# More blocks of 512 rows: 21 singles, 48 pairs, then 22 blocks of four units, 18 of them beside the remaining conv and route work

## The chip, the cores and the metric

The kernel runs on one NeuronCore of a Trainium2 chip. A core has a matrix engine (TensorE, PE in the profile), a vector engine (VectorE, DVE), an activation engine (ScalarE, ACT), a general engine [...] (GpSimd, POOL), and SyncE (SP), which issues the plain DMAs. [...] The metric is device time in microseconds. Everything is float32.

## What is computed

The input is 8 sequences of 3,584 rows with 192 channels, 28,672 rows in all. First comes a causal convolution along the sequence with 7 taps and 8 heads of 24 channels; each head's taps are a softmax of its 7 weights. Then each row goes to one of 8 experts:

```python
logits = x @ w_gate; local_gate = sigmoid(x @ w_local)
for each row s of a sequence:
    fresh = argmax(logits[s])
    e = fresh if s == 0 or local_gate[s] < 0.5 else previous e
    p = softmax(logits[s])
    out[s] = p[e] * (relu(x[s] @ w1[e]) @ w2[e])
```

`w1[e]` is 192 x 1024 and `w2[e]` 1024 x 192. A row whose local gate is not below 0.5 keeps the expert of the row before it, so the expert is a scan along the sequence.

## The kernel before

**Groups and slots.** The rows are handled in 16 groups of 1,792 (`PT`, `NPART`). For a group, conv makes the convolved rows `y_sb` (one ScalarE multiply for the first tap of a head, six VectorE multiply-adds for the others, L401 and L411). Route then computes logits, experts, probabilities and, for each row, its slot in a DRAM table `slots`, in which every expert has a region of its own. Groups 0 and 1 are done in a faster way with matmuls at the start (`wide`, `wide_route`). Each group's rows are scattered to their slots by 14 indirect DMAs of 128 rows (`put`, L801) that GpSimd issues; 16 of them for groups 0 and 1.

**Blocks.** The expert network runs over blocks of rows of one expert. A unit is 128 rows (`UT`). A block has one unit ("single"), two ("pair", `BT`) or four (`QT`, 512 rows). While groups are still arriving, the kernel takes as many full blocks as the rows that have arrived must yield whatever their experts are (`_sure`), and a bit more in the late stages (`_likely`). The lists `ONE` and `TWO` say up to which block each group serves: 35 singles, all from groups 0 to 2 (`EARLY = 3`), then 60 pairs from groups 3 to 12 (`PAIRED = 60`). After the last group come 13 blocks of four, 4 late pairs, 14 late singles that take what is left of each expert, and spare blocks, which are run only when a planned block found no rows. `FIRST` is the number of the first block of four, 95. The tables that say which expert and which unit a block has are computed on VectorE (`table`, `tables`) and read by SyncE (`entry`).

**One block.** SyncE loads the expert's weights, 1.5 MB, three blocks ahead (`load_w`, four buffers), and the rows of the block from the slots (`load_rows`). TensorE transposes the rows (`turn`, L383), ScalarE copies them to SBUF; TensorE does the hidden product (`hidden`, L999), ScalarE applies relu; TensorE does the second product (`output`, L1016), ScalarE and VectorE scale and add its two halves (L1024, L1030), and GpSimd scatters the rows to `out` (L1034). TensorE's order is: hidden of this block, transposes of the next, output of this block.

**Blocks of four.** Their hidden product (`seven`, L1152) is a two-by-two scheme of Strassen's kind over two row halves and two of the three 64-channel thirds: 7 products in place of 8, with the remaining third done plainly, so 11 half-size products in place of 12. It needs sums of weights (`combine_w`, four on GpSimd) and of rows (`combine_x`, five on VectorE), three copies out of PSUM on ScalarE (h11, h22, h12), and three sums of 128 x 1,024 on VectorE (L1166, L1169, L1179). The second product (`output_late`, L1196) has two parts of 256 rows. In this stage PSUM is divided anew: the pools of the pair stage are closed (`banks.close()`), and three double banks `late_p` take their place. The buffers for xT, the combinations and h come from the conv's input and row tiles (`make_room`), since conv is over by then.

**Side work.** Conv and route of the coming groups are written as Python generators that yield an assumed cost after each instruction. Between the parts of a block the kernel calls `step(time)`, which adds instructions of route, or of conv where there is no route work or route has yielded "hop", until the assumed costs add up to `time`: for a pair 4.8 after the hidden product, 1.2 within the output and 3.6 after it. `ensure(i)` issues the row loads of up to three blocks ahead; while a group that block needs is not routed or not fully scattered, and the block is at most two ahead, it adds a step of 4.2 and a `put` at once. Elsewhere `put(ins)` makes GpSimd wait for the instruction `ins` ("anchor"), which spaces the scatters.

Of the kernel before, what the change touches and what calls it, by code (L numbers as in the profile page):

```python
# [17 lines left out]
P = 128  # L18
# [28 lines left out]
EARLY = 3  # L47
# [17 lines left out]
PAIRED = 60  # L65
LEFT4 = E * (QT // 2 + UT // 8)
LEFT2 = E * (BT // 2 + UT // 8)
# [3 lines left out]
PAST = ONE[-1] * UT + TWO[-1] * BT  # L71
FOUR = _likely(N - PAST, QT, LEFT4)
LOST = FOUR - _sure(N - PAST, QT)
# [7 lines left out]
REST = NU - ONE[-1] - 2 * TWO[-1] - 4 * FOUR - 2 * PAIRS + LOSE  # L81
# [21 lines left out]
def kernel(  # L103
# [14 lines left out]
    ys = ctx.enter_context(tc.tile_pool(name="ys", bufs=4))  # L118
# [5 lines left out]
    hp = ctx.enter_context(tc.tile_pool(name="hp", bufs=1))  # L124
    op = ctx.enter_context(tc.tile_pool(name="op", bufs=2))
# [244 lines left out]
    tab = [cst.tile([P, 3], F32, name=f"tab{k}") for k in range(5)]  # L370
    ends = [cst.tile([P, 1 + E], F32, name=f"ends{k}") for k in range(5)]
    for k in range(5):
        nc.gpsimd.memset(tab[k], 0.0)
        nc.gpsimd.memset(ends[k], 0.0)
# [12 lines left out]
    def row_tile():  # L387
        return ys.tile([P, NB, DG], F32, name="y_sb")

    def conv(g, x_sb):  # L390
        y_sb = row_tile()[:, :NT, :]
# [197 lines left out]
    def logits(g, y_sb):  # L589
# [6 lines left out]
        yield "hop"  # L596


        lps = [hps_p.tile([P, TQ * Q], F32, name="hps") for half in range(2)]
# [15 lines left out]
        for r in range(4):  # L615
            for j in range(4):
                t, u = TQ * j, min(TQ * (j + 1), NT)
                at = r // 2 * TQ + t - begin[j]
                e0 = r % 2 * (E + 1)
                nc.vector.tensor_copy(lt[Q * r:Q * r + Q, t:u, :],  # L620
                                      lq[Q * j:Q * j + Q, at:at + u - t, e0:e0 + E + 1])
                yield 0.12
        return lt

    def route(g):
# [62 lines left out]
        krow = sm.tile([1, 2, P], F32, name="krow")  # L688
# [89 lines left out]
    def tables(g):  # L778
        if ONE[g] > (ONE[g - 1] if g else 0):
            yield from table(0, g, 1, ONE[g])  # L780
        if TWO[g] > (TWO[g - 1] if g else 0):
            yield from table(1, g, 2, TWO[g])
        if g == LAST:
            yield from table(2, g, 4, FOUR, 0)
            yield from table(3, g, 2, PAIRS, 0)
            yield from table(4, g, 1, None)
            yield from fill(g)
# [133 lines left out]
    blocks += [(2, 4, i, LAST) for i in range(FOUR)]  # L921
    blocks += [(3, 2, i, LAST) for i in range(PAIRS)]
    blocks += [(4, 1, i, PADS) for i in range(REST)]

# [39 lines left out]
    def turn(n, xg):  # L964
# [9 lines left out]
        xT = tp.tile([P, KD, BT], F32, name="xT")  # L974
# [13 lines left out]
    def hidden(n, wb, xT, shares=(1, 1)):  # L988
# [4 lines left out]
        for two in range(2):  # L993
            hps = [hps_p.tile([P, 2, BT], F32, name="hps") for half in range(2)]
            for d in range(KD):
                for j in range(2):
                    f0 = (d * 4 + two * 2 + j) * P
                    for half, rows in halves():
                        nc.tensor.matmul(hps[half][:, j, w], lhsT=wb[rows, f0:f0 + P],  # L999
                                         rhs=xT[rows, d, w], start=(d == 0 and j == 0),  # L1000
                                         stop=(d == KD - 1), skip_group_check=True)
# [3 lines left out]
            for _ in range(shares[two] if n == KT else (0, sum(shares))[two]):  # L1005
# [3 lines left out]
    def output(n, wb, xg, hT):  # L1009

        yps = [yps_p.tile([P, 512], F32, name="yps") for half in range(2)]
        for m4 in ([0, 1, 4, 5], [2, 3, 6, 7]):
            for k in range(n):
                for m in m4:
                    for half, rows in halves():
                        nc.tensor.matmul(yps[half][:, k * D:(k + 1) * D],  # L1016
                                         lhsT=hT[rows, m, k * P:(k + 1) * P],
                                         rhs=wb[rows, WA + m * D:WA + (m + 1) * D],
                                         start=(m == 0 and k == 0), stop=(m == FK - 1),
                                         skip_group_check=True)  # L1020
        o_sb = op.tile([P, KT, D], F32, name="o_sb")
        y = [[yps[half][:, k * D:(k + 1) * D] for half in range(2)] for k in range(n)]
        for k in range(n):
            half = nc.scalar.activation(o_sb[:, k, :], y[k][0], Act.Copy, scale=xg[:, k, 0:1])  # L1024
        if n == KT and len(to_put) > NT - 2:
            put(half)

        step(1.2 if n > 1 or st["block"] else 0)
        for k in range(n):
# [3 lines left out]
            nc.gpsimd.nop()  # L1033
            sent = nc.gpsimd.indirect_dma_start(  # L1034
                out=out, in_=o_sb[:, k, :], in_offset=None,
                out_offset=bass.IndirectOffsetOnAxis(ap=xg.bitcast(I32)[:, k, IX:], axis=0),
                bounds_check=N - 1, oob_is_err=False)
            tc.declare_no_dep(sent.ins, group="sent", reason="each token has one slot")
            tc.add_to_no_dep_group("sent", sent.ins)
# [4 lines left out]
    def ring(i):  # L1044

        if "rows" not in room:
            room["rows"] = row_tile().rearrange("p b d -> p (b d)")
# [3 lines left out]
    def make_room():  # L1051

        one, two = [xs.tile([P, NX, D], F32, name="x_sb").rearrange("p t d -> p (t d)")
                    for _ in range(2)]
        three = row_tile().rearrange("p b d -> p (b d)")
        for name, flat, at, size in (("xT", one, 0, KD * QT), ("xc", one, KD * QT, 4 * HU * P),
                                     ("wt", one, KD * QT + 4 * HU * P, 6 * P),
                                     ("h0", two, 0, 4 * HU * P), ("h1", two, 4 * HU * P, 4 * HU * P),
                                     ("h2", two, 8 * HU * P, 4 * HU * P), ("h3", three, 0, 4 * HU * P)):
            room[name] = flat[:, at:at + size]  # L1060
# [13 lines left out]
    def turn_in(n, at):  # L1074
        xT = room["xT"][:, :KD * n * P].rearrange("p (d s) -> p d s", d=KD)
# [34 lines left out]
    def combine_w(wb):  # L1110


        wt = room["wt"].rearrange("p (k s) -> p k s", k=3)
# [396 lines left out]
```

## Time and profile before

| | us |
|---|---|
| median of 3 runs | 1322.66 (1322.0 to 1323.66) |
| the profiled execution, its own time | 1305.35 |
| its span | 1303.6 |
| TensorE busy (matmul) | 1284.2 |
| VectorE busy | 846.3 |
| ScalarE busy | 651.1 |
| GpSimd busy | 523.1 |
| first block of four starts at | 910.24 |
| last block of four ends at | 1175.6 |

The span is from the first to the last instruction; the profiled execution's own time has 1.75 us more around it. Busy time of TensorE is modelled, so 99% does not mean that each matmul runs at its peak. The page's slices divide the span in 40 parts of 32.6 us with the busy share in tenths. Line numbers are those of the kernel before.

### The profile page before, as it was taken

The page shows a single profiled execution, that of the slowest core. Times are in us where ns is not written, and L with a number is a line of the kernel's source. Part 1 is how long each engine was busy: PE and PEld are TensorE (multiplying, and loading weights), DVE is VectorE, ACT ScalarE, POOL GpSimd, SP SyncE. Part 2 cuts the span into 40 slices and gives each one's busy share as a digit, 9 for nine tenths or more (in the row PEclk, how much of TensorE's full clock was granted, in tenths as well). Part 3 has the DMA queues.
Part 4 walks back from the last instruction along what each step waited for, and adds up shares of the span by engine and source line. Part 5 has one row for each costly group of instructions (what it writes and reads, how often), then busy time and mean ns, then how long its engine had stood idle before and what let it go on. Part 6 is the DMA issues. An engine that isn't in the chain of part 4 may idle for free.

```text
span 1303.6 us, 40830 instructions
## 1 busy us (share of the span) xinstructions
PE 1284.2 (99%) x16434; PEld 1220.6 (94%) x16434; DVE 846.3 (65%) x2526; ACT 651.1 (50%) x1482; POOL 523.1 (40%) x577
## 2 busy tenths in 40 slices
PE   9899999999999999999999999999999999999997
PEld 7799999999999999999999999999999999999997
DVE  5989898988988899998999996801333333330000
ACT  5456565544445445444454544444645556454453
POOL 3455353533435344353544534454433433322211
PEclk9999999999999999999999999999999999999999
DMA  5799999975757576575765755666323323324584
GB/s 195 285 357 415 386 384 345 398 273 202 269 203 278 196 274 244 207 280 190 281 246 204 281 193 205 214 213 235 128 87 135 122 105 140 110 94 167 212 303 164
DMA packets 63077, 300.42 MB, mean 230 GB/s; under 512 B 12064, under 2 KB 34263, under 8 KB 45474
## 3 DMA queue, kind: packets, MB, share of 16 engines
q1 hardware_dynamic: 40560, 252.54, 53.2%
q0 software_dynamic: 22320, 45.22, 9.5%
q8 instruction: 131, 2.15, 0.7%
q14 instruction: 64, 0.52, 0.1%
q10 hardware_dynamic: 2, 0.00, 0.0%
HBM read 252.12 MB, written 46.07 MB: 229 GB/s over the span
## 4 chain that ended last, share of the span: by engine, by line
PE 96%; DVE 3%; issue 0%; POOL 0%; POOLq 0%; ACT 0%; DVEq 0%
PE yps L1016 31%; PE hps L999 31%; PE ps L1196 15%; PE ps L1152 8%; PE ps L1103 4%; PE xps L383 2%; PE xps L1152 2%; PE hps L604 2%; DVE y_sb L411 1%; PE hps L233 1%; PE hps L178 0%; DVE hot L574 0%; PE hps L256 0%; PE yps L264 0%; DVE run L475 0%
## 5 line engine op out<-in xcount | busy, mean ns | idle before, releaser
L1016 PE MATMUL yps<-wb,hT 64*128 64x192 f32 x4960 | 429.8, 325 | 3.2 <-DVE o_sb L1030 2.4
L999 PE MATMUL hps<-xT,wb 64*128 64x256 f32 (+1 forms) x4560 | 425.9, 338 | 1.9 <-DVE at L503 1.2
L999 PEld LDWEIGHTS hps<-xT,wb 64*128 64x128 f32 x4560 | 378.7, 188 | 33.9 <-issue 3.9
L1016 PEld LDWEIGHTS yps<-wb,hT 64*128 64x128 f32 x4960 | 405.7, 187 | 4.6 <-DVE o_sb L1030 2.7
L411 DVE SCALAR_TENSOR_TENSOR y_sb<-x_sb,c,y_sb 128x336 f32<-128x336 f32 x672 | 375.6, 569 | 28.4 <-ACT y_sb L401 10.5
L801 POOL DMA_INDIRECT slots<-y_sb,posi x228 | 229.6, 1007 | 205.7 <-ACT xT L985 90.8
L1004 ACT ACTIVATE hT<-hps 128x512 f32<-128x512 f32 (+1 forms) x380 | 176.4, 516 | 244.5 <-PE hps L999 244.5
L1034 POOL DMA_INDIRECT out_dram<-o_sb,xg x155 | 161.5, 1042 | 276.0 <-DVE o_sb L1030 222.2
L1209 DVE SCALAR_TENSOR_TENSOR o_sb<-ps,y_sb,o_sb 128x192 f32<-128x192 f32 x74 | 28.1, 413 | 233.5 <-ACT o_sb L1206 233.5
L1214 POOL DMA_INDIRECT out_dram<-o_sb,y_sb x74 | 76.4, 1032 | 237.5 <-DVE o_sb L1209 218.7
L1196 PE MATMUL ps<-wb,x_sb 64*128 64x192 f32 x1952 | 165.0, 323 | 0.0
L1196 PEld LDWEIGHTS ps<-wb,x_sb 64*128 64x128 f32 x1952 | 159.3, 187 | 0.6
L1024 ACT ACTIVATE o_sb<-yps,xg 128x192 f32<-128x192 f32 x155 | 58.7, 418 | 178.4 <-PE yps L1016 178.3
L985 ACT COPY xT<-xps 128x256 f32<-128x256 f32 (+3 forms) x380 | 142.0, 374 | 10.6 <-PE xps L383 4.8
L1030 DVE SCALAR_TENSOR_TENSOR o_sb<-yps,xg,o_sb 128x192 f32<-128x192 f32 x155 | 58.6, 410 | 77.2 <-ACT o_sb L1024 77.0
L1206 ACT ACTIVATE o_sb<-ps,y_sb 128x192 f32<-128x192 f32 x74 | 27.9, 418 | 102.2 <-PE ps L1196 97.7
L1152 PE MATMUL ps<-x_sb,wb 64*128 64x256 f32 x624 | 73.7, 376 | 0.0
L1152 PEld LDWEIGHTS ps<-x_sb,wb 64*128 64x128 f32 x624 | 59.0, 187 | 7.3
L401 ACT ACTIVATE y_sb<-x_sb,c 128x336 f32<-128x336 f32 x112 | 61.9, 578 | 0.0
L1103 PE MATMUL ps<-x_sb,wb 64*128 64x128 f32 (+1 forms) x864 | 61.6, 295 | 0.0
L1103 PEld LDWEIGHTS ps<-x_sb,wb 64*128 64x128 f32 x864 | 59.4, 188 | 0.9 <-issue 0.2
L1083 ACT COPY x_sb<-xps 128x128 f32<-128x128 f32 (+5 forms) x124 | 58.7, 473 | 2.3
(277 smaller groups left out, 1043.5 us busy)
## 6 DMA issues: line engine op xcount, KB each, us to landing
wb<-in_w_dram SPq DMA_DIRECT2D x122, 1536.0 KB
x_sb<-in_x_dram SPq DMA_DIRECT2D x14, 1920.0 KB
xg<-slots SPq DMA_DIRECT2D x60, 195.0 KB
wb<-in_w_dram SPq DMA_DIRECT2D x12, 512.0 KB
y_sb<-slots SPq DMA_DIRECT2D x13, 390.0 KB
slots<-y_sb,posi POOLq DMA_INDIRECT x228
xg<-slots SPq DMA_DIRECT2D x33, 97.5 KB
x_sb<-in_xb_dram SPq DMA_DIRECT2D x4, 768.0 KB
```

The lines of the kernel that those rows point to most:

```text
L401: nc.scalar.activation(cols(h), chans(h, 0), Act.Copy, scale=c[:, h, 0:1])
L411: nc.vector.scalar_tensor_tensor(cols(h), chans(h, k), c[:, h, k:k + 1], cols(h), Alu.mult, Alu.add)
L801: ins = nc.gpsimd.indirect_dma_start(out=slots[:, :], in_=rows, in_offset=None, out_offset=bass.IndirectOffsetOnAxis(ap=to, axis=0)).ins
L985: copied = nc.scalar.copy(a, b)
L999: nc.tensor.matmul(hps[half][:, j, w], lhsT=wb[rows, f0:f0 + P], rhs=xT[rows, d, w], start=(d == 0 and j == 0), stop=(d == KD - 1), skip_g ...
L1004: relu = nc.scalar.activation(hT[:, m:m + 2, w], hps[half][:, :, w], Act.Relu)
L1016: nc.tensor.matmul(yps[half][:, k * D:(k + 1) * D], lhsT=hT[rows, m, k * P:(k + 1) * P], rhs=wb[rows, WA + m * D:WA + (m + 1) * D], start= ...
L1034: sent = nc.gpsimd.indirect_dma_start(out=out, in_=o_sb[:, k, :], in_offset=None, out_offset=bass.IndirectOffsetOnAxis(ap=xg.bitcast(I32)[ ...
L1103: nc.tensor.matmul(hps[:, half, j, :], lhsT=wb[rows, f0:f0 + P], rhs=xT[rows, d, :], start=(d == 0 and j == 0), stop=(d == KD - 1), skip_g ...
L1152: ins = nc.tensor.matmul(to[:, half, j, :], lhsT=b[rows, j * P:(j + 1) * P], rhs=a[rows, :], start=(first and j == 0), stop=True, skip_gro ...
L1196: ins = nc.tensor.matmul(yps[:, half, k * D:(k + 1) * D], lhsT=h[two][rows, side, j, k * P:(k + 1) * P], rhs=wb[rows, WA + f * D:WA + (f + ...
L1214: sent = nc.gpsimd.indirect_dma_start(out=out, in_=o_sb[:, k, :], in_offset=None, out_offset=bass.IndirectOffsetOnAxis(ap=xg.bitcast(I32)[ ...
```

## The change

The plan of blocks changes. `EARLY` goes from 3 to 2 and `PAIRED` from 60 to 48, so there are 21 singles (groups 0 and 1) and 48 pairs (groups 2 to 9). A new list `MID` gives 18 blocks of four from groups 10 to 14, with a table of their own (kind 2), and only 4 of the blocks of four wait for the last group. After them come 5 late pairs and 14 late singles. The whole is 21 + 48 + 22 + 5 + 14 blocks in place of 35 + 60 + 13 + 4 + 14. `FIRST` is 69.

Conv and route of groups 13 to 15 are therefore still under way in the stage of blocks of four. `step` is called there too, with the shares `SIDE = (2.4, 4.6, 1.7, 1.5)`: ahead of the h11 sum, after the transposed copies, and after the row scaling on ScalarE in parts 0 and 1. Route's logits on TensorE are then put between parts 0 and 1 and use the bank `late_p[0]`; a new yield "pe" holds them back until such a place comes, and there are none in the last pair ahead of that stage. The overrun of a step is carried to the next (`over`). The 16 small copies of logits into `lt` move from VectorE to ScalarE, four at a time with a "hop" after each four. The order of the built program has these four ScalarE copies between the row scaling of part 1 and the next block's h11 copy three times.

The second row scatter of a pair, or of each part of a block of four, is no longer issued at once: it is kept in `held` and issued with an anchor on a later TensorE instruction. Some scatters to `slots` get other anchors. Row loads in a block of four are issued inside `seven` (`rows_then`).

Buffers: the row tiles `ys` become four named pools, three of them used from group 8 on, so that the fourth holds the rows of the blocks of four; xT has one pool for all stages; h comes from the tile `hot` of the start; the combinations come from five row tiles `xg` and, for two of them, from `hT` after its last use (`more_room`).

```diff
-EARLY = 3
+EARLY = 2
-PAIRED = 60
+NARROW = 8
+PAIRED = 48
+LEFTM = E * (QT // 2 + UT // 2)
+MID = [_likely((g + 1) * PT - PAST, QT, LEFTM) if TWO[g] == TWO[-1] else 0
+       for g in range(LAST)]
+PAST += MID[LAST] * QT
...
+    def row_tile(g):
+        at = g % 4 if g < NARROW else (g + 1) % 3
+        return ys[at].tile([P, NB, DG], F32, name="y_sb")
...
-        yield "hop"
-        lps = [hps_p.tile([P, TQ * Q], F32, name="hps") for half in range(2)]
+        yield "pe"
+        if late_p:
+            both = st["bank"].tile([P, 2, 512], F32, name="ps")
+            lps = [both[:, half, :TQ * Q] for half in range(2)]
+        else:
+            lps = [hps_p.tile([P, TQ * Q], F32, name="hps") for half in range(2)]
...
-                nc.vector.tensor_copy(lt[Q * r:Q * r + Q, t:u, :],
-                                      lq[Q * j:Q * j + Q, at:at + u - t, e0:e0 + E + 1])
-                yield 0.12
+                nc.scalar.copy(lt[Q * r:Q * r + Q, t:u, :],
+                               lq[Q * j:Q * j + Q, at:at + u - t, e0:e0 + E + 1])
+            yield "hop"
...
+        if MID[g] > (MID[g - 1] if g else 0):
+            yield from table(2, g, 4, MID[g], MID[g - 1])
...
+                        if held and d:
+                            held.pop(0)(ins)
...
+            if k == 0:
+                deliver(o_sb[:, 0, :], xg, 0)
+            else:
+                held.append(lambda ins, k=k: deliver(o_sb[:, k, :], xg, k, ins))
...
+        if behind is not None:
+            tc.add_manual_dep(sent.ins, behind.ins.name, SYNC, reason="scatters apart")
...
-        times(yb, s1, t1, True)
+        ins = times(yb, s1, t1, True)
+        if held:
+            held.pop(0)(ins)
+        rows_then()
...
         times(wbk, a13, b31)
+        if st["block"] > FIRST:
+            step(SIDE[0], early=1)
         nc.vector.tensor_tensor(h11, wbk, h11, op=Alu.add)
...
+            if n == KQ:
+                step(SIDE[2 + part], late_p[0] if part == 0 else None)
...
+        if st["due"]:
+            go = (not late_p and st["block"] < FIRST - 1
+                  or bank is not None and (force or st["since"] < st["block"]))
...
+        time += st["over"]
...
             while st["routed"] < g or any(p[0] <= g for p in to_put):
                 if j > i + 2:
                     return
-                step(4.2)
+                if st["routed"] < g:
+                    step(4.2, late_p[0] if late_p else None, force=True)
                 put()
...
+        if n == KQ:
+            step(SIDE[1])
```

## The prediction

> **What bounds the kernel now.** I read the page first: busy shares, the slices, the chain that ended last. Then the TensorE timeline in three windows, then every engine inside one block of 512 rows.
>
> ```profile
> PE 1284.2 (99%) x16434; PEld 1220.6 (94%) x16434; DVE 846.3 (65%) x2526; ACT 651.1 (50%) x1482; POOL 523.1 (40%) x577
> ...
> PE   9899999999999999999999999999999999999997
> ...
> DVE  5989898988988899998999996801333333330000
> ...
> PE 96%; DVE 3%; issue 0%; POOL 0%; POOLq 0%; ACT 0%; DVEq 0%
> ```
>
> TensorE sets the end from slice 2 to the last. VectorE is close behind it for 24 slices (conv and route) and nearly free afterwards. So a change is worth the TensorE time it removes, less the new waits it puts in front of TensorE. What one block costs is the distance between equal lines of the TensorE timeline: singles, pairs, blocks of 512.
>
> ```profile
> 103.42 2.86 PE L999 MATMUL hps<-xT,wb 64*128 64x128 f32 x48
> ...
> 108.87 2.86 PE L999 MATMUL hps<-xT,wb 64*128 64x128 f32 x48
> ...
> 790.90 5.35 PE L999 MATMUL hps<-xT,wb 64*128 64x256 f32 x48
> ...
> 801.56 5.34 PE L999 MATMUL hps<-xT,wb 64*128 64x256 f32 x48
> ...
> 930.66 2.75 PE L1152 MATMUL ps<-x_sb,wb 64*128 64x256 f32 x24
> ...
> 951.08 2.75 PE L1152 MATMUL ps<-x_sb,wb 64*128 64x256 f32 x24
> ```
>
> A single is 5.445 us (four of them from 92.53 to 114.31), a pair 10.67, a block of 512 rows 20.42 against 21.34 for two pairs: it makes 11 products where plain multiplication makes 12. The last view is the inside of such a block (its start is 971.49).
>
> ```profile
> 972.62 1.01 ACT L1158 COPY x_sb<-ps 128x1024 f32<-128x1024 f32 x1 [0.18 <-PE ps L1152]
> ...
> 974.08 1.03 PE L1152 MATMUL ps<-x_sb 64*128 64x256 f32 x8
> ...
> 976.96 1.22 DVE L1166 TENSOR_TENSOR x_sb<-xps,x_sb 128x1024 f32<-128x1024 f32 x1 [3.74 <-PE xps L1152]
> ...
> 978.17 1.23 DVE L1169 TENSOR_TENSOR y_sb<-ps,y_sb 128x1024 f32<-128x1024 f32 x1
> ...
> 979.26 0.63 PE L383 MATMUL xps<-ident,y_sb 64*128 64x64 f32 x16
> ...
> 979.73 1.08 PE L1152 MATMUL ps<-x_sb 64*128 64x256 f32 x8
> ```
>
> Three handovers are narrow. ScalarE's copy of h11 ends at 973.63, and the product into that bank starts at 974.08: 0.45 us to spare. VectorE's h11 sum ends at 978.18, before the transposes at 979.26: 1.08. Its h22 sum ends at 979.40, before 979.73: 0.33. Today nothing else runs on those engines then; after the change conv and route do.
>
> [...] an early row load issued at 53.98 freed TensorE at 56.03, and the scatter whose row ends at 80.45 released its reader only at 87.20, 6.75 us later, with the DMA engines full. [...]
>
> **The change, part by part.**
>
> *Blocks.* 14 singles go (35 to 21), 12 pairs go (60 to 48), 9 blocks of 512 come (13 to 22), one late pair comes (4 to 5). Rows agree: 1,792 + 3,072 = 4,608 + 256. TensorE: −14×5.445 − 12×10.67 + 9×20.42 + 10.67 = −76.2 − 128.0 + 183.8 + 10.7 = **−9.8 us**. The 14 logits passes on TensorE (1.7 us each) stay.
>
> *Blocks that find no rows.* An expert table with too few full units would give an empty block of 20.42 us. Worked out on the given inputs, groups 10 to 14 offer 5, 9, 13, 14 and 20 blocks against 4, 7, 11, 14 and 18 planned: none is empty. 0.
>
> *Side work beside the blocks of 512.* VectorE per block of 512: its own 3×1.22 + 5×0.44 + 4×0.41 = 7.5; side work by SIDE 10.2 units, some 17 conv ops of 0.585 (7 ops took 4.07 at 655.10), 9.9. Sum 17.4 of 20.42. Followed in order: h12 sum ends 9.2 after the block's start; 11 conv ops to 15.6; row sums of part 0 ready at 16.2, done 16.9; five combinations to 19.1; three conv ops to 20.9; next block: row sums to 1.7, four conv ops to 4.1; the h11 sum is due at 5.5. It is idle again 1.4 us before the narrow place, so the cover holds. If not, each us late beyond 0.33 is a us of TensorE. I take 1.0 us for the whole stage (18 blocks, and the first, where conv stands between the combinations and the last pair's row sums); bounds 0 and 9 (one conv op of 0.585 ahead of the sum, in 15 blocks).
>
> *Logits copies on ScalarE.* Per group 16 copies leave VectorE (3.47 us at 649.72). On ScalarE the trace has none; [...] the nearest row (ls, 128x128) is 0.27. In the built order four of them stand between the row scaling of part 1 and the h11 copy in three blocks (groups 13, 14, 15): [...] 0.5 each, **+1.5 us**; bounds 1.3 and 2.0. Before singles and pairs they stand behind the transposed copies, with over 1 us free on ScalarE (2.76 idle at 670.29): 0.
>
> *EARLY 2.* Pairs start at row 2,688, so rows of group 3 are needed from row 3,456 in place of 4,480. In the built order nine scatters of group 3 still wait when block 22 begins, and are issued without an anchor, one after the other, because block 24's rows need them all. GpSimd, from the start T of block 22: row scatter of block 21 at T+1.35 (263.30 to 264.65 in this trace), 0.99 long, gap 0.30; nine at 1.25 pitch (29.81, 31.06, 32.30) end at T+13.6. [...] load and its landing 2.05: T+17.7. TensorE turns these rows at T+10.67+5.18 = T+15.85. Wait 1.8; I take **+2.2** for SP's issue. Bounds: 0.8 (landing in 1) and 6.5 (landing in 6.75). Behind SP's waiting load stand block 25's rows and weights; the weights go out about T+17 for use at T+34, after some 4 us: no second wait. Behind the nine on GpSimd is block 21's second row scatter, which nobody needs before block 23's row scaling. Block 29 has six: [...] bounds 0 and 2.8.
>
> *Spaced scatters, pools, pair steps.* The second scatter of a block now waits on GpSimd for a TensorE instruction. GpSimd in a full block of 512: up to six puts and four scatters at 1.27 and four combinations at 0.75, 15.7 of 20.42; weight combinations end about 18.5 after the block's start, first used 21.3 after. The ring's row loads have three blocks. Hand-over to the new stage without logits in the last pair, transposed tile from its own pool, combination buffers from free row tiles: 0, covered by the same slack.
>
> Sum: −9.8 + 2.2 + 1.5 + 1.0 = **−5.1 us**. The profiled execution took 1305.35, its span 1303.6; the span becomes 1298.5. The median of the runs is 1322.66, 17.3 above the profiled one; that gap I cannot place and carry over: **1317.5 us**, −0.39%. About 0.2% (2.6 us) is what a measurement of this kernel can tell from no change.
>
> **Rivals.**
> 1. *Full gain.* The nine scatters land in time, copies slip through: −9.8 + 0.3, 1313.2. For: the waits view lists only 10 us for TensorE in the whole run. Against: T+17.7 is past T+15.85.
> 2. *Landing under load.* Scatters land in 6.75: 6.5 at block 22, 2.8 at block 29; −9.8 + 9.3 + 2.5 = +2.0, 1324.7. For: the 6.75 was in the single stage, which ends one block before. Against: SP holds weight loads back meanwhile, so the queues empty.
> 3. *Slower: VectorE late for the h11 sum.* If two conv ops (1.17) stand ahead of it when the bank is ready, the h22 sum is 0.84 past its slack; over 15 blocks 12.6, with the 3.7 above: +6.5, 1329.2. It decides from 0.41 us a block ((9.8−3.7)/15). For: VectorE at 85% of the block, three narrow handovers. Against: the 1.4 us counted above.
> 4. *It does not do what it says* (empty blocks): 20.42 each; excluded by the count, 0.
>
> **How the numbers follow.** Forecast 0.48 (own range 1315 to 1320), rival 1 0.20, rival 2 0.18, rival 3 0.14. Faster by over 0.2%: 0.48 + 0.20 = 0.68. Within: 0.18 (rival 2). Slower: 0.14. The range from rival 1's lower edge to rival 2's: 1312.5 to 1325; it leaves out rival 3 and a little.
>
> **What would show it.** In the changed profile: 20.4 us between the starts of most mixed blocks; one TensorE wait of about 2 us for a row load at its transposes, in the third pair after the singles; three waits of about 0.5 at the fourth product for ScalarE; VectorE idle before the h11 sum. Wrong if TensorE waits for VectorE in most mixed blocks, if pairs or singles lengthen from 10.67 and 5.445, or if the chain shows a DMA of several us.

## The result, and the profile after

The changed kernel took 1337.62 us (median of five runs, 1337.13 to 1339.40). Beside it the kernel before took 1323.66 (1322.00 to 1328.92). The ratio is 1.0103, with a 95% interval of 1.0080 to 1.0126: slower by 1.0%, where the forecast was 0.4% faster.

One thing has to be said first, because no number below can be read without it. The experiments ran on six chips, and these are of two kinds. On three of them the kernel before takes 1305 us, and its traces show no hold-up of the kind described below. On the other three it takes 1325 to 1333, and there the other engines are held up for short times, mostly while GpSimd issues scatters. The profile of before that the forecast was read from (1305.35) is of the first kind; the medians of before (1322.66 and 1323.66) and everything measured in this section are of the second. On the first kind the changed kernel is 0.2% *faster*.

The page of the changed kernel, busy shares, slices and the chain that ended last:

```profile
PE 1299.6 (97%) x16026; PEld 1261.5 (94%) x16026; DVE 893.6 (67%) x2427; ACT 716.1 (54%) x1605; POOL 550.7 (41%) x615
...
PE   8899998999999999999999999999999999999997
...
DVE  6878885868878888888888888877647643320000
...
PEclk9999998989989999999999999999999999999999
...
POOL 0%; POOLq 0%
```

TensorE is still the busy engine. But its row has an 8 in slice 7, where before had 9 from slice 3 to the last but one, and the granted clock (`PEclk`, in tenths of full speed) has an 8 in slices 7, 9 and 12. The chain says nothing this time: it stops at the last scatter. Next, block lengths in the TensorE timeline, as before: two singles, two pairs, two blocks of 512.

```profile
164.93 2.84 PE L1016 MATMUL hps<-xT,wb 64*128 64x128 f32 x48
170.38 2.84 PE L1016 MATMUL hps<-xT,wb 64*128 64x128 f32 x48
...
527.64 5.34 PE L1016 MATMUL hps<-xT,wb 64*128 64x256 f32 x48
538.31 5.34 PE L1016 MATMUL hps<-xT,wb 64*128 64x256 f32 x48
...
1012.02 2.79 PE L1186 MATMUL ps<-xT,wb 64*128 64x256 f32 x24
...
1032.44 2.79 PE L1186 MATMUL ps<-xT,wb 64*128 64x256 f32 x24
```

5.45, 10.67 and 20.42: undisturbed blocks cost what they cost before, and side work on VectorE does not lengthen a block of 512. The first block of 512 starts at 739.5; by the forecast's own sum it should have been 700.9 (910.2 - 76.2 - 128.0 - 5.1, the last for three logits passes that moved behind this point). From there to the end it takes 5 us more than the same sum says. So, measured against the undisturbed trace of before that the sum starts from, nearly 39 us were lost ahead of it, all but 1 in singles and pairs. Three pairs stand out: block 22 is 19.15 us long, block 29 15.94, block 36 17.48, where 10.67 is normal. TensorE in block 22 (the last number is the idle time before the line, and what ended it):

```profile
198.71 3.09 PE L1035 MATMUL yps<-wb,hT 64*128 64x192 f32 x24
202.21 0.43 PE L1035 MATMUL yps<-wb,hT 64*128 64x192 f32 x2 [0.41 <-issue]
202.91 0.32 PE L1035 MATMUL yps<-wb,hT 64*128 64x192 f32 x1 [0.27 <-issue]
203.63 0.60 PE L1035 MATMUL yps<-wb,hT 64*128 64x192 f32 x4 [0.40 <-issue]
205.04 0.80 PE L1035 MATMUL yps<-wb,hT 64*128 64x192 f32 x3 [0.81 <-issue]
206.47 1.02 PE L1035 MATMUL yps<-wb,hT 64*128 64x192 f32 x4 [0.63 <-issue]
208.60 3.13 PE L1035 MATMUL yps<-wb,hT 64*128 64x192 f32 x15 [1.10 <-issue]
```

This is no wait for rows. TensorE is in the middle of an output product whose inputs are all there, and gets one to four matmuls every 0.71 us or a multiple of it. GpSimd in the same time:

```profile
199.03 0.96 POOL L816 DMA_INDIRECT slots<-y_sb,posi  x1 [0.30 <-DMA slots<-y_sb,posi]
200.29 0.96 POOL L816 DMA_INDIRECT slots<-y_sb,posi  x1 [0.30 <-DMA slots<-y_sb,posi]
201.56 0.96 POOL L816 DMA_INDIRECT slots<-y_sb,posi  x1 [0.31 <-issue]
202.82 0.96 POOL L816 DMA_INDIRECT slots<-y_sb,posi  x1 [0.30 <-issue]
204.08 0.96 POOL L816 DMA_INDIRECT slots<-y_sb,posi  x1 [0.30 <-issue]
205.35 0.96 POOL L816 DMA_INDIRECT slots<-y_sb,posi  x1 [0.30 <-issue]
206.61 0.98 POOL L1062 DMA_INDIRECT out_dram<-o_sb,xg  x1 [0.30 <-issue]
```

Eleven scatters follow each other from 193.62 to 207.59 with 0.3 us between them: the nine unanchored ones of block 22 and a row scatter on each side. The trickle begins while the sixth is issued and ends a us after the last. Blocks 29 and 36, where unanchored scatters join the row scatters in runs of eight and seven, look the same: it begins during the sixth and the fifth, 6.9 and 5.3 us after the first. Then comes a second loss. The view of all engines by stretch (third column from the end: the granted clock):

```profile
192.30:203.00 10.70, 9.79 (x97) 8.65 (x94) 7.59 (x13) 4.69 (x10) 7.25 (x8) 1.00 0.19 65
203.00:214.00 11.00, 8.02 (x40) 7.02 (x41) 1.88 (x4) 1.66 (x4) 4.66 (x5) 0.57 0.54 172
```

When the trickle begins TensorE still has its full clock. From 204.5 on the clock is 0.5 for 10 us, so the next hidden product takes 7.06 us in place of 5.35. The waits view of the changed kernel, TensorE's rows, shows the rest of the loss:

```profile
PE yps L1035 <- issue: 10.8, 18, 1.1
PE yps L1035 <- ACT hT L1023: 4.9, 8, 1.4
```

Beyond their length without a disturbance, the three pairs and the slow blocks behind them cost 8.5 + 1.6 + 5.3 + 1.3 + 6.8 = 23.5 us. The other 15 of the 39 us are not broken down; no wait of TensorE in this view is above 2.0 us.

### The profile page after: what moved, and what is told of

Read it like the earlier page. It is cut to its first block, busy times and chain, and to the rows that moved or that the text cites. A ratio compares the mean times of both kernels' runs of the same rounds, so it can differ in the third digit from the quotient of the medians.

```text
span 1337.6 us, 39934 instructions
## 1 busy us (share of the span) xinstructions
PE 1299.6 (97%) x16026; PEld 1261.5 (94%) x16026; DVE 893.6 (67%) x2427; ACT 716.1 (54%) x1605; POOL 550.7 (41%) x615
## 5 line engine op out<-in xcount | busy, mean ns | idle before, releaser
L1035 PE MATMUL yps<-wb,hT 64*128 64x192 f32 x3744 | 344.6, 330 | 18.5 <-issue 10.8
L1035 PEld LDWEIGHTS yps<-wb,hT 64*128 64x128 f32 x3744 | 315.9, 189 | 31.8 <-issue 21.7
L1016 PE MATMUL hps<-xT,wb 64*128 64x256 f32 (+1 forms) x3312 | 328.4, 347 | 2.1 <-DVE at L512 1.2
L1016 PEld LDWEIGHTS hps<-xT,wb 64*128 64x128 f32 x3312 | 307.9, 189 | 10.5 <-issue 1.9
L1235 PE MATMUL ps<-wb,hot 64*128 64x192 f32 x3584 | 301.8, 323 | 0.1
L1235 PEld LDWEIGHTS ps<-wb,hot 64*128 64x128 f32 x3584 | 293.7, 187 | 1.6 <-issue 1.5
L1023 ACT ACTIVATE hT<-hps 128x512 f32<-128x512 f32 (+1 forms) x276 | 132.4, 529 | 153.7 <-PE hps L1016 99.0
L1002 ACT COPY xT<-xps 64x256 f32<-64x256 f32 (+4 forms) x276 | 105.4, 382 | 18.2 <-remote 11.4
L1116 ACT COPY xT<-xps 64x512 f32<-64x512 f32 (+6 forms) x164 | 85.0, 518 | 2.3
L1186 PE MATMUL ps<-xT,wb 64*128 64x256 f32 x704 | 84.7, 376 | 0.0
L1186 PEld LDWEIGHTS ps<-xT,wb 64*128 64x128 f32 x704 | 74.3, 187 | 0.9
L1136 PEld LDWEIGHTS ps<-xT,wb 64*128 64x128 f32 x912 | 65.1, 188 | 2.3 <-issue 1.3
(282 smaller groups left out, 1337.6 us busy)
```

Source lines behind the costliest of these rows:

```text
L1002: copied = nc.scalar.copy(a, b)
L1016: ins = nc.tensor.matmul(hps[half][:, j, w], lhsT=wb[rows, f0:f0 + P], rhs=xT[rows, d, w], start=(d == 0 and j == 0), stop=(d == KD - 1), ...
L1023: relu = nc.scalar.activation(hT[:, m:m + 2, w], hps[half][:, :, w], Act.Relu)
L1035: ins = nc.tensor.matmul(yps[half][:, k * D:(k + 1) * D], lhsT=hT[rows, m, k * P:(k + 1) * P], rhs=wb[rows, WA + m * D:WA + (m + 1) * D], ...
L1116: copied = nc.scalar.copy(a, b)
L1136: nc.tensor.matmul(hps[:, half, j, :], lhsT=wb[rows, f0:f0 + P], rhs=xT[rows, d, :], start=(d == 0 and j == 0), stop=(d == KD - 1), skip_g ...
```

## The experiments

### The chip: the changed kernel and the kernel before, again

No edit. The kernel before had taken 18 us more beside the result than in the profile that I had read.

> The changed kernel itself, a second time. The kernel before took 1323.7 us beside the first runs of the changed kernel and 1305.6 beside the experiments, 18 us less, and with the copies alone put back on VectorE the pair with nine scatters shows no hold-up at all. Theory 5, the hold-ups of TensorE during scatters belong to the circumstances of the execution and not to the program: where the kernel before takes 1305, this one takes 1304.9 plus what the copies on ScalarE cost in singles and pairs (5 to 9 us), 1309 to 1314, without the three long pairs. Theory 1b, they belong to the program, and the copies on ScalarE are part of their cause: 1335 to 1340 again, with the three long pairs.

> The kernel before, as a run with its own profile. Theory 5: 1303 to 1308 with a span near 1303.6 and no hold-ups, as its first profile; a trace of about 1320 would show where its slower runs lose 17 us.

Measured on one chip: changed 1301.71 us, before 1304.85, ratio 0.9977 (0.9970 to 0.9983); the copy of before 1304.90, ratio 1.0000 (0.9991 to 1.0008). The same program that took 1337.6 takes 1301.7. Its blocks 22 and 23 (TensorE, SyncE's DMA issue and GpSimd in one timeline):

```profile
187.72 5.43 PE L1035 MATMUL yps<-wb,hT 64*128 64x192 f32 x64
...
192.97 5.36 PE L1016 MATMUL hps<-xT,wb 64*128 64x256 f32 x48
...
196.66 0.98 POOL L1062 DMA_INDIRECT out_dram<-o_sb,xg  x1 [0.30 <-issue]
...
198.01 1.23 SPq L963 DMA_DIRECT2D xg<-slots  x2
...
200.63 0.45 PE L391 MATMUL xps<-ident,xg 64*128 64x64 f32 x8 [2.30 <-DMA xg<-slots]
```

Here too the nine scatters follow each other in block 22, from 184.94 to 196.36, with one row scatter right ahead of them and three right behind, thirteen in a row, and TensorE goes on as if there were none: its products have their full number of matmuls without a break (x64, x48). What is there instead is the wait that I had forecast: for the rows of block 24, in block 23, 2.30 us long. So the hold-ups are no property of the program alone, as theory 5 says. The time is 7 us below the 1309 to 1314 that I had expected with it: I had counted 5 to 9 us for the copies on ScalarE in singles and pairs, and no such loss came.

> The changed kernel a third time, to see on what the hold-ups depend. If they belong to the chip: where the kernel before takes about 1305, this takes 1299 to 1304; where it takes about 1323, this takes about 1337 with long pairs at blocks 22, 29 and 36 and register moves of 0.3 to 0.7 us on SyncE (29 ns in the undisturbed trace). If they come and go on one chip: some runs of both kinds.

> The changed kernel a fourth time. Chip with hold-ups: ratio to before 1.006 to 1.014, three long pairs. Undisturbed chip: ratio 0.997 to 0.999.

The third time another chip was met: 1338.37 against 1324.70, ratio 1.0103 (1.0065 to 1.0142), with block 22 at 19.51 us, 29 at 16.92, 36 at 17.08. The fourth time 1301.86 against 1304.79, ratio 0.9980 (0.9971 to 0.9989). Kernels run together on one chip were always of one kind, so it goes with the chip or with what it did at that hour. One chip, an undisturbed one, was met twice, 19 minutes apart, and was undisturbed both times; that is too little to tell the two apart. That other work on the chip crowds the DMA engines is not what the traces show: by the pages, the packets of GpSimd's queue take 9.4% of 1337.6 us in the result and 9.7% of 1299.4 in the undisturbed run, the same 126 us.

The stages by chip, as distances of first matmuls in the TensorE timeline (us; before and changed on one undisturbed chip, then before and changed on chips with hold-ups, which aren't the same chip: before takes 1332.86 on the one and 1323.66 on the other):

| | before, undisturbed | changed, undisturbed | before, held up | changed, held up (the result) |
|---|---|---|---|---|
| up to the first block | 43.7 | 43.7 | 46.2 | 45.8 |
| singles (35 / 21) | 206.2 | 128.0 | 222.2 | 135.6 |
| pairs (60 / 48) | 657.6 | 530.6 | 669.4 | 558.1 |
| blocks of 512 (13 / 22) | 265.2 | 455.0 | 265.3 | 457.1 |
| late pairs and singles | 128.0 | 142.1 | 130.5 | 141.0 |
| span | 1300.7 | 1299.4 | 1333.6 | 1337.6 |

A chip with hold-ups costs time where rows are scattered to their slots, in singles and pairs, and little afterwards. It costs the kernel before time as well.

> The kernel before with its own trace. Undisturbed chip: 1303 to 1306, no register move of SyncE above 0.1 us. Chip with hold-ups: 1322 to 1326, some twenty such moves, and 18 us of short waits of TensorE in singles and pairs, no pair above 13.5 us.

> The kernel before with its own trace. Chip with hold-ups: 1322 to 1335, register moves of 0.3 to 0.7 us on SyncE, 18 us or more of short hold-ups, no pair above 13.5 us, and no run of more than four scatters in pairs. Undisturbed chip: 1303 to 1306, no such moves.

The third trace of before is of an undisturbed chip (1305.04, ratio 1.0003), the fourth of one with hold-ups (1332.86, ratio 0.9997). The longest pair in the fourth is 12.55 us, one with a logits pass. TensorE's waits there, matmuls first, then the rows of its weight loads:

```profile
PE yps L1016 <- issue: 3.5, 6, 0.9
PE hps L604 <- issue: 3.4, 10, 0.4
...
PEld yps L1016 <- issue: 7.9, 21, 1.0
PEld hps L604 <- issue: 6.8, 14, 0.6
PEld hps L999 <- issue: 6.6, 22, 0.5
```

Many short ones, no long one. The clearest mark of such a chip is on SyncE, whose register moves wait for nothing that the trace shows. The moves of the line that loads weights, in the result and in the undisturbed run (shortest, median and longest in ns, then the first and last start):

```profile
L956 SPq MOVE wb<-in_w_dram x118: 3/29/707, 34.0 to 1311.8; - x118
...
L956 SPq MOVE wb<-in_w_dram x118: 29/29/38, 33.3 to 1272.4; - x118
```

Of all 228 moves in the result 22 take 0.13 to 0.71 us; in the twelve traces from undisturbed chips none is above 0.1. Taking moves and register operations of eight traces with hold-ups together, 190 of 3,788 are above 0.1, and 75% of these begin inside a scatter's row on GpSimd, where 33% of all begin. So instructions for which the trace shows no wait are held up, mostly while GpSimd issues a scatter. The other engines have idle time that nothing in the trace ends: from 60 to 1150 us TensorE 12.4 us, ScalarE 26.4 and VectorE 3.0 in the result, against 0, 5.6 and 0 in the undisturbed run. GpSimd's own 231 moves are not held up; none is above 0.04 us.

### The runs of scatters: taken away, broken up, multiplied

First the changed kernel with 35 singles and 41 pairs, so that no scatter is issued without an anchor:

```diff
-EARLY = 2
+EARLY = 3
-PAIRED = 48
+PAIRED = 41
```

> The changed kernel with 35 singles and 41 pairs again (the same 14,976 rows), all else as changed; no scatter of rows is issued without an anchor any more. Theory 1, back-to-back scatters (TensorE is held up while GpSimd issues six and more scatters without a break, and then runs at half clock): the three long pairs (18.98, 15.73, 17.48 us and the slow blocks after them) are gone, 23 us less; 14 singles for 7 pairs cost 14 x 5.445 - 7 x 10.67 = 1.5 more; about 1316. Theory 2, the moved copies and held scatters lengthen the pairs whatever the queue holds: the long blocks stay, about 1339. Theory 3, late rows (my forecast's step): only the 2 us wait goes, about 1337.

> The changed kernel with 35 singles and 41 pairs once more: no unanchored scatter, no run of more than three scatters in pairs. Chip with hold-ups: the three long pairs (23 us together) are gone, and what is left of the changed kernel's loss is the short hold-ups of singles and pairs that the old division showed as well: ratio to before 0.993 (only the long runs matter) to 1.004 (the short ones remain as in the old division, 11 us). Undisturbed chip: 0.997 to 0.999, as the first time.

Undisturbed chip: 1303.17 us, ratio 0.9980 (0.9971 to 0.9989), as the changed kernel itself: the 1.5 us that the plan costs and the 2.3 us of the row wait nearly cancel. The theories could not be told apart there, since on that chip there was nothing to explain. Chip with hold-ups: 1333.67, ratio 1.0006 (0.9994 to 1.0017), where the changed kernel has 1.0103. No pair is above 13.7 us, and the clock never falls before the last blocks (its mean is 0.998). So about 13 us go with the three runs, less than the 23.5 that they cost. The plan itself costs 1.5, and the 14 singles more are held up in their turn: they take 91.4 us there against 82.3 undisturbed, 9.1 more. 23.5 - 1.5 - 9.1 is 12.9, which fits. What is left in its pairs are short runs, nine of four in a row; I had expected none above three.

Then more scatters per block, so that less is left over at block 22:

```diff
-            hT = hidden(n, wbs[i], xT, (1, 1) if i else (0, 0))
+            hT = hidden(n, wbs[i], xT, (3, 3) if i else (0, 0))
```

and, in the second pair of runs, `(3, 3) if i > 19 else (1, 1) if i else (0, 0)`: from the end of the singles on only.

> The changed kernel, 21 singles and 48 pairs, but with three scatters of rows behind each relu in place of one, so that the queue is short when block 22 begins (2 left there, none at blocks 29 and 36), and no run of scatters is longer than about four. Theory 1: the three long pairs are gone although EARLY stays 2, about 1337.6 - 23 = 1315; the runs of three or four cost at most 1 us per group, 1315 to 1322. Theory 2: no gain, 1335 or more.

> The changed kernel with three scatters of rows behind each relu from block 20 on (in place of one), the singles before it as they are; two unanchored scatters are left at block 22, none at 29 and 36. On an undisturbed chip: the wait of 2.0 to 2.3 us for the rows of block 24 goes, 2 to 3 us less than the changed kernel, ratio to before 0.995 to 0.997. On a chip where scatters hold up the other engines (register moves of 0.3 to 0.7 us): the three long pairs go if it takes six and more scatters in a row to starve TensorE, 20 us less, 1315 to 1320; if every scatter costs the same wherever it stands, 1336 to 1340 as before.

> The changed kernel with three scatters behind each relu from block 20 on, once more. Chip with hold-ups: the three long pairs are gone if only six and more scatters in a row starve TensorE, ratio to before 0.992 to 0.999 in place of 1.010; ratio 1.008 to 1.012 if every scatter costs the same wherever it stands. Undisturbed chip: 0.994 to 0.997, as the first time.

In singles too (undisturbed chip, so the expectation was not put to the test): 1306.81, ratio 1.0004 (0.9994 to 1.0014). In its trace the pairs gain 2.7 us and the singles lose 10 (138.1 in place of 128.0), with 7.2 us of waits for the relu; but the traced execution took 1312.44, the longest of the thirteen, so the usual loss is smaller. Why was not followed up. From block 20 on (undisturbed chip): 1299.72, ratio 0.9954 (0.9940 to 0.9969). The row wait of block 23 is gone, and this version beats both kernels there. On a chip with hold-ups the very same kernel took 1423.81, ratio 1.069 (1.066 to 1.072). My expectation was wrong in its premise: three scatters behind each relu don't stay three. A pair then has six of them and two row scatters, and eight at 1.27 us are 10.2 of its 10.67 us, so one follows the other. On the undisturbed chip they stand in runs of up to eighteen, 23.6 us long, and TensorE has no idle time in any of them. On the chip with hold-ups TensorE's stops break them into runs of six and seven. GpSimd's timeline there, then TensorE's:

```profile
322.52 1.06 POOL L816 DMA_INDIRECT slots<-y_sb,posi  x1 [1.40 <-issue]
...
326.41 0.96 POOL L816 DMA_INDIRECT slots<-y_sb,posi  x1 [0.30 <-issue]
327.68 0.96 POOL L816 DMA_INDIRECT slots<-y_sb,posi  x1 [0.30 <-issue]
328.94 0.99 POOL L1062 DMA_INDIRECT out_dram<-o_sb,xg  x1 [0.30 <-DVE y_sb L420]
```

```profile
324.67 4.36 PE L1016 MATMUL hps<-xT,wb 64*128 64x256 f32 x35
329.77 0.71 PE L1016 MATMUL hps<-xT,wb 64*128 64x256 f32 x4 [0.74 <-issue]
331.21 0.46 PE L1016 MATMUL hps<-xT,wb 64*128 64x256 f32 x1 [0.73 <-issue]
```

Here TensorE trickles after the fifth in a row. It does so in every group, mostly in two pairs of 14 to 20 us, with half clock twelve times ahead of the last blocks (the mean granted clock is 0.972); in the other runs of six and seven, all but one, it begins between the third scatter and the sixth, 2.7 to 6.5 us after the first. The edit had made the runs that it was to remove, and so it became the best evidence for them: same program, 1299.7 us where a run of scatters costs TensorE nothing, 1423.8 where it does. That every scatter costs the same wherever it stands is refuted, since the number of scatters is that of the changed kernel. The length of a run alone does not decide either: sixteen runs of four in the pairs of the fourth trace of before cost TensorE at most 0.9 us each, and one of five beside the blocks of 512 of the result (744.3 to 750.6) stops nothing.

Last, a pause of about 1 us (six fills of a scratch tile, of which five take 0.98 us in the trace) ahead of each unanchored scatter:

```diff
+                if i < FIRST:
+                    for _ in range(6):
+                        nc.gpsimd.memset(pause, 0.0)
                 put()
```

> The changed kernel with six short fills of a scratch tile on GpSimd ahead of each scatter that is issued without an anchor, about 1 us of pause for each (ahead of the first as well). Chip with hold-ups: if TensorE is starved because the scatters follow without a break, its trickle in the three long pairs is gone and it waits for the late rows of block 24 instead (about 9 us later than without the pause, so 9 to 11 us of wait there, 4 to 8 at block 29), the loss to the half clock included about the same total; if the number of scatters alone counts, trickle and wait add up, 8 to 15 us above the changed kernel. Undisturbed chip: 9 us at block 22 and 3 to 6 at block 29 added, 1312 to 1318.

It met an undisturbed chip, so whether a pause frees TensorE stays open: whether the number of scatters or the lack of a break between them does it, no run shows. It did test the forecast's step, though: 1320.14, ratio 1.0129 (1.0110 to 1.0148), 18.3 us above the changed kernel beside it and above the 1312 to 1318 that I had expected. TensorE's waits and the row load, in the waits view and the timeline:

```profile
PE xps L392 <- DMA xg<-slots: 17.7, 3, 11.7
```

```profile
209.65 1.23 SPq L964 DMA_DIRECT2D xg<-slots  x2
...
212.16 0.69 PE L392 MATMUL xps<-ident,xg 64*128 64x64 f32 x8 [11.65 <-DMA xg<-slots]
```

Pauses that delay the load move TensorE's wait from 2.2 to 11.65 us, and a second one of 4.65 us comes behind the run of block 29. The logits pass behind the first wait takes 2.63 us, behind the wait of 2.30 in the changed kernel 1.59, and the mean granted clock is 0.992, in the changed kernel beside it 0.996. In all, the two pairs are 10.7 and 6.5 us longer than in the changed kernel, 17.2 of the 18.3 us. So the row load behind the run is what TensorE waits for, as forecast.

### The copies on ScalarE

```diff
-                nc.scalar.copy(lt[Q * r:Q * r + Q, t:u, :],
-                               lq[Q * j:Q * j + Q, at:at + u - t, e0:e0 + E + 1])
+                copy = nc.scalar.copy if late_p else nc.vector.tensor_copy
+                copy(lt[Q * r:Q * r + Q, t:u, :],
+                     lq[Q * j:Q * j + Q, at:at + u - t, e0:e0 + E + 1])
```

> The changed kernel with the 16 logits copies of a group on VectorE again while singles and pairs run, on ScalarE only beside the blocks of 512; the order of all instructions is otherwise kept. Theory 4, that the copies on ScalarE hold up the relus: TensorE's waits for the relu of the singles (0.5 to 1.4 us each, six of them) and about 0.85 us once per group go, 4 to 10 us less, 1328 to 1334; the three long pairs stay. Rival: the copies' time on VectorE (about 3.5 us per group) comes back as waits for it, 1337 or more.

> The changed kernel with the logits copies on VectorE until the blocks of 512, once more. Undisturbed chip: ratio to before 0.998 to 1.000, as the first time. Chip with hold-ups: the old division of rows with the new code was 11 us slower than before there, without any long run of scatters; if that is the copies' doing (ScalarE, held up at each scatter, gets to the relus late), this takes 1325 to 1330, with the three long pairs still there; if not, 1336 or more.

> As the run beside it, and the logits copies on VectorE while singles and pairs run. Chip with hold-ups: 8 to 11 us less than the run beside it if the copies on ScalarE are what the new code lost there with the old division; the same or more if not. Undisturbed chip: 3 us more than the run beside it, since there the copies on VectorE cost 1304.9 in place of 1301.7.

Undisturbed chips: 1304.90 (ratio 0.9993, 0.9985 to 1.0001) and 1304.94 (1.0000, 0.9990 to 1.0009), 2 to 3 us above the changed kernel by the ratios. The waits view, TensorE:

```profile
PE yps L1036 <- DVE o_sb L1050: 4.4, 5, 1.9
PE xps L391 <- DMA xg<-slots: 3.8, 2, 2.0
```

VectorE now gets late to the row sums of singles, 132.4 us for 21 of them in place of 128.0 and 129.1. So moving the copies to ScalarE is worth 2 to 3 us by itself, in singles. On a chip with hold-ups this was tested only together with the three scatters per relu: with the copies on VectorE 1435.06 in place of 1423.81, 11 us more, not 8 to 11 less. In the pairs the runs of scatters differ between these two, but in the singles ahead of them they don't, and there the copies on VectorE take 138.1 us against 136.2. So nothing is seen of a loss by the copies, and theory 4 finds no support; the changed kernel itself was not run that way on such a chip, where all waits for the relu are 4.9 us. Theory 1b had fallen with the first undisturbed run.

### The other parts

Two more versions: the changed code with the old division of rows, and the changed kernel with no scatter held for an anchor:

```diff
-EARLY = 2
+EARLY = 3
-PAIRED = 48
+PAIRED = 60
-MID = [_likely((g + 1) * PT - PAST, QT, LEFTM) if TWO[g] == TWO[-1] else 0
-       for g in range(LAST)]
+MID = [0] * LAST
```

```diff
-            if k == 0:
-                deliver(o_sb[:, 0, :], xg, 0)
+            if True:
+                deliver(o_sb[:, k, :], xg, k)
...
-                if k == 0 or n < KQ:
+                if True:
```

> The changed code with the old division of rows: 35 singles, 60 pairs, 13 blocks of 512 after all side work, 4 late pairs. My sum gives the new code by itself 0 (copies on ScalarE, spaced scatters, pools), so the time of the kernel before, ratio 0.999 to 1.001. Rival: the copies on ScalarE take 3.5 us per group off VectorE and shorten the pairs, 2 to 4 us faster than before, and the new division then brings next to nothing.

> The changed kernel with every scatter of results issued as soon as its rows are summed, none held for a TensorE instruction. My sum says 0: the time of the changed kernel within 1 us. Rival: the spacing keeps the transfers of rows from being late, and without it the changed kernel loses 2 us or more.

Both were run on a chip with hold-ups only. Without holding scatters: 1337.48, ratio 1.0092 (1.0063 to 1.0120), the changed kernel's 1.0103 within the intervals: 0, as I had it. The new code with the old division: 1336.10, ratio 1.0092 (1.0062 to 1.0122), without any run of scatters longer than four in pairs, and with the full clock until the last blocks (its mean is 0.998). So on that chip the new code by itself lost 11 us, which I had not expected. Which of its parts does it is not settled: neither the copies nor the held scatters showed a loss in the kernels in which they were tested. And as a trace of before from the same chip is missing, the 11 us can't be placed either; the trace of before from another such chip, where before itself is 8 us slower, has the same singles (222.2 against 223.9) and pairs (669.4 against 668.6). A part of it need not be hold-up at all: on the undisturbed chips the 35 singles take 211.4 us in the new code (with 41 pairs) and 206.2 to 207.9 in the code before.

The kernel before with the singles of the change:

```diff
-EARLY = 3
+EARLY = 2
-PAIRED = 60
+PAIRED = 67
```

> The kernel before with 21 singles and 67 pairs in place of 35 and 60, nothing else: its copies stay on VectorE and no scatter is held. Seven scatters wait when block 22 begins and go out one after the other. Theory 1: one long pair there, 4 to 8 us, and a block at half clock, 1.5 us; less 14 x 5.445 - 7 x 10.67 = 1.5 that the pairs save: 4 to 8 us slower than before. Theory 2: 1.5 us faster than before, no long pair.

Undisturbed chip: 1326.89, ratio 1.0160 (1.0143 to 1.0177), 21 us slower than before, which neither theory had. It is another thing (waits view, TensorE; then VectorE's timeline):

```profile
PE hps L604 <- DVE z L594: 13.1, 2, 12.9
```

```profile
182.94 10.79 DVE L411 SCALAR_TENSOR_TENSOR y_sb<-x_sb,c,y_sb 128x336 f32<-128x336 f32 x18
193.76 3.16 DVE L594 STREAM_TRANSPOSE z<-y_sb 128x768 f32<-128x768 f32 x4
```

In the old code each forced scatter also forces a slice of conv and route, even when the rows are routed: seven slices at block 22. They put 18 conv operations ahead of the transposes that the logits pass needs, and TensorE runs nothing for the 12.9 us until they are done. The change puts `if st["routed"] < g` ahead of that slice, and in the changed kernel the same wait is 0.3 us. I had not priced it at all.

## Why the prediction was wrong

The sum was made against a profile in which nothing is held up, and on chips of that kind it was right in sign and near in size: -5.1 us forecast, -3.1 and -2.9 measured. On the chips that the result is from it was wrong by 19 us. Step by step:

- **Blocks, -9.8.** Held. Lengths of 5.445, 10.67 and 20.42 are in every trace. In the table the stage of 512 grows by 189.8: 9 x 20.42, three logits passes of 1.75 and 0.66.
- **EARLY 2, +2.2 for a late row load.** Held on undisturbed chips: the load was issued 15.7 us after the start of block 22, the wait was 2.30, 2.2 and 2.04. The landing time of the scatters in that sum was my own estimate, which the trace of before did not show: it had a plain load of SyncE's queue (2.05 us) and one scatter (6.75, with the DMA engines busy for 0.84 of it). Here the last of the nine ends at 196.36 and the load that waits for it is issued at 198.01, 1.65 us later; from 182.3 to 193 the DMA engines are busy for 0.22 of the time, in the 10.3 us before for 0.99. Block 29: 0, as forecast. On a chip with hold-ups this step failed. I priced nine scatters in a row by when they land, and took TensorE's own work to go on beside them. In place of 2.2 us at one block there were 23.5 at three, and of another kind. My own sign of being wrong, pairs longer than 10.67, is what came.
- **Logits copies, +1.5 in blocks of 512, 0 in singles and pairs.** The 0.5 a block was my own estimate, which no row of the trace of before shows; by the nearest row, 0.27, four copies are 1.08 against 0.45 to spare, 0.63 a block. Measured: a copy takes 0.22 us (0.89 for four), and three blocks are 0.22 longer, 0.66 in all; and in singles one relu wait of 1.2 us where I had 0. Against VectorE, where they were, they gain 2 to 3 us.
- **VectorE beside blocks of 512, +1.0.** Measured 0. VectorE waits 2.3 us on average for the bank of the h11 sum (50.7 us over 22), more than the 1.4 that I had followed by hand. Rival 3 had the right sign and a mechanism that never appears.
- **Late stage, 10.67 for one pair more.** Measured 13 to 14: two late singles take 6.7 and 6.5 us in place of 5.44, the one by a wait of 1.06 for its weights, the other by 0.89 on an instruction of SyncE, which I had not looked at.
- **"That gap I cannot place and carry over."** This is the step that turned the sign. Medians of before lay 17.3 us above its profiled execution. I added the gap as a constant. It was the time that chips with hold-ups take, and it depends on the program: 19 us of before (1323.66 - 1304.85) and 36 of the changed kernel (1337.62 - 1301.71). My range, 1312.5 to 1325, took in nothing for it.

On the chips with hold-ups the account is not closed. The -3.1 us of an undisturbed chip, less the row wait of 2.3, which isn't there where TensorE is late anyway, plus 23.5 make 18.1, and 14.0 was measured. Fewer singles and pairs to be held up may be the 4 us between, which is not shown; the 11 us that the new code lost with the old division find no room in this sum.

What was right, then, is the mechanism on the undisturbed chip. Its total is in part luck: 1.8 us too much for copies and VectorE in the blocks of 512 stand against some 4 too little for the late stage and the singles. What was missing is a second cost of scatters in a row, of which the trace of before showed no sign, and the readiness to see one in an unexplained gap of 1.3%.

## What to carry to other kernels

When the profiled execution is faster than the median by more than the runs scatter, the profile lacks something that the runs have; find it before you price a change, or let the range hold it. In this kernel, scatters from GpSimd are better spread than bunched even where a bunch costs nothing in the trace at hand: the version with three per relu won 0.5% on one chip and lost 7% on another, while the one without any unanchored scatter (35 singles, 41 pairs) was 0.2% faster on the one kind and level on the other, the best of those tried on both. And an edit that raises a rate must be followed to the queue: three per relu became eighteen in a row on the one kind of chip, and seven, with TensorE's stops between, on the other.

## What the runs showed of the hardware

On some chips the other engines' instructions are held up while GpSimd issues scatters, SyncE's register moves (29 ns, then up to 0.71 us) as well as TensorE's matmuls. Runs of six and more, 21 of the 22 in the result and the version with three per relu, brought TensorE down to a few matmuls per 0.71 us, from the third to the sixth scatter on, 2.7 to 7.1 us after the first; in the result its clock fell to 0.5 another 2.2 to 3.8 us later, all three times, for 10.2, 6.8 and 6.8 us. On other chips eighteen in a row, 23.6 us, do nothing of the kind.

What the hold-up is was not found. A delay in the queue q8 (128 packets in the result, 2.10 MB by its page) does not go with TensorE's stops: its packets take 0.97 us in the median in the result and 0.98 in the undisturbed run, and leave at nearly the same instruction of TensorE in both. In block 22 one came at 192.1 and the next at 211.0, after TensorE had recovered at 208.6.
